# A gated attention and mixer block: token mixing's first product with tokens as the stationary side, and its result turned round by transposes and DRAM

## The chip, the cores and the metric

The kernel runs on one core of one Trainium2 chip. The metric is the device time of one execution in microseconds (us), lower is better. The kernel before takes 911.43 us (median of 3 runs, 911.35 to 912.27).

A core has a matrix engine (PE, with its weight loads shown apart as PEld), a vector engine (DVE), an activation engine (ACT), a general engine (POOL) and a sync engine (SP). In this kernel SP does nothing but issue DMA transfers, one after the other. Every engine works through its own list of instructions in order, and they meet through semaphores: an instruction that waits holds up all that stand behind it on its engine.

## The reference

One input `x` of 2048 tokens by 448 channels goes through attention (16 heads, one shared key and value head) and through a mixer, and a gate adds the two. What matters here is the first half of the mixer, token mixing:

```python
h = _gelu(_layernorm(x, axis=-1) @ w1)
c = D // 4
g0 = jnp.pad(h[:, :, 0*c:1*c], ((0, 0), (1, 0), (0, 0)))[:, :S, :]   # shift +1
g1 = jnp.pad(h[:, :, 1*c:2*c], ((0, 0), (0, 1), (0, 0)))[:, 1:, :]   # shift -1
g2 = jnp.pad(h[:, :, 2*c:3*c], ((0, 0), (2, 0), (0, 0)))[:, :S, :]   # shift +2
g3 = jnp.pad(h[:, :, 3*c:   ], ((0, 0), (0, 2), (0, 0)))[:, 2:, :]   # shift -2
hs = jnp.concatenate([g0, g1, g2, g3], axis=-1) @ w2
x1 = x + hs
...
h2 = _gelu(_layernorm(x1, axis=-1) @ w3) @ w4
```

S is 2048, D is 448 and c is 112. Each quarter of the channels of `h` is moved by one or two tokens before it meets `w2`. All is float32.

## The kernel before, in words

The program has three parts in order of time: token mixing together with the projections of queries, keys and values (to about 124 us), channel mixing with w3 and w4 (to about 400 us), and attention (the rest). The change lies in the first part alone.

Tokens are worked in four blocks of 512 (b = 0 to 3). To keep float32 accuracy at the speed of one pass, each operand is split into a high and a low part (`ah`/`al`, `w1h`/`w1l`, `hh`/`hl`), and a product is made of three, high by high, high by low and low by high. The 448 channels fill three groups of 128 rows and a fourth of 64 that carries another part's rows in its upper half, so a product over the channels takes 11 matmuls (`proj`, lines 129 to 135).

- `stage_q` (u = 0 to 15) projects queries, with keys, values and the gate in spare columns, and sends the result through ACT to DRAM (`q_out`, DRAM tensor `qd`). `stage_kv(b)` issues two loads that bring values back from there (`vT`), and `stage_v` turns all of them by four PE transposes (`vp`) after the first tile of `stage_w2(2)`.
- `stage_w1(b)` makes `h` with channels on the partitions: w1 is the stationary side (112 columns, one quarter m of the channels) and 512 tokens stream past. DVE multiplies the result by the reciprocal deviation of each token. These factors lie along the free dimension, so they have to be spread over the partitions: `ln1_send` transposes them on PE (`rsT`) and writes them to DRAM, `ln1_read` reads them back on 112 partitions (`rsb`). The layernorm's mean is already taken out through w1 (`centre_w1`). ACT then makes the gelu twice, once rounded into `hh` and once in full, and POOL subtracts for `hl`.
- `carry_h(b)` issues seven small DMA transfers on SP that put 16 rows of `hl` at a time into the upper 16 partitions (112 to 127) of `hh` and `hl`, where they save a separate product.
- `stage_w2(b)` makes `hs` for four tiles t of 128 tokens, 11 matmuls each of 448 columns with the tokens of `hh`/`hl` as stationary side, shifted by reading at another offset. DVE adds the result to `x1`. The results rest in two PSUM banks, used in turn (`hs_tile`), so the third tile waits for the first one's addition. The two columns beyond a block come from the next block's `hh` and `hl`, copied by POOL.

`hh` and `hl` have two buffers each. Large temporaries of this part (`xkv`, and later `xn4` and `xt4`) share three buffers under the tag "raw" in turn. During `stage_w2(1)` DVE also makes the layernorm of the first block for channel mixing (`xn4`, turned into `xt4`), `xt_write(0)` sends it to DRAM (`xd`) with four transfers, and `xt_read(0)` brings it back with channels on the partitions (`xr`).

The order on every engine is the order of the code (a manual schedule). For PE it is w1(0), w1(1), w2(0), w1(2), w2(1), q(12 to 15), w1(3), w2(2), w2(3), and then the first w3 group.

Of the kernel before, what the change touches and what calls it, by code (L numbers as in the profile page):

```python
# [37 lines left out]
def f32(ap):  # L38
    return ap.bitcast(F32)
# [3 lines left out]
def gated_mix_kernel(  # L43
# [206 lines left out]
    with tc.tile_pool(name="s1b", bufs=1) as s1b, \  # L250
# [43 lines left out]
        def high_x(b, c0, c1):  # L294
            if b not in xact:
                xact[b] = (s1.tile([P, 4, 512], F32R, tag="ah", bufs=3, name=f"ahk_{b}"),
                           s1.tile([P, 3, 512], F32R, tag="al", bufs=3, name=f"alk_{b}"))
            nc.scalar.copy(xact[b][0][:, c0:c1, :], xraw[b][:, c0:c1, :])

# [61 lines left out]
        rb_of = {}  # L361

# [8 lines left out]

        def ln1_send(b):
            ps = misc_tile(f"rsT_{b}")[0:4, 0:P]
            nc.tensor.transpose(ps, rs1_of.pop(b)[1], ident)
            rT = s1.tile([4, P], F32, tag="rT", bufs=2, name=f"rT_{b}")
            nc.scalar.copy(rT, ps)
            rb_of[b] = dram.tile([4, P], F32, tag="rsd", bufs=2, name=f"rsd_{b}")
            nc.sync.dma_start(rb_of[b], rT)

        def ln1_read(b):  # L380
            rd = rb_of[b]
            rb_of[b] = s1.tile([P, 512], F32, tag="rsb", bufs=2, name=f"rsb_{b}")
            nc.sync.dma_start(rb_of[b][0:C], rd.rearrange("(o t) p -> o (t p)", o=1).broadcast_to([C, 512]))
# [42 lines left out]

        def stage_w1(b, between=None):
            hh[b] = s1b.tile([P, 4, 516], F32R, tag="hh", bufs=2, name=f"hh_{b}")
            hl[b] = s1b.tile([P, 4, 516], F32R, tag="hl", bufs=2, name=f"hl_{b}")
            for tt in (hl, hh):  # L430
                if b == 0:
                    nc.gpsimd.memset(f32(tt[b])[0:C, :, 0:2], 0.0)
                else:
                    nc.gpsimd.tensor_copy(tt[b][0:C, :, 0:2], f32(tt[b - 1])[0:C, :, 512:514])
            for i, m in enumerate(ORDER):
                ps = mm1(f"h_{b}_{m}")
                w = slice(m * C, (m + 1) * C)
                proj(ps[0:C, :], w1h[:, :, w], w1l[:, :, w], *xact[b])
                if between:
# [4 lines left out]
                nc.scalar.activation(hf[0:C, :], hf[0:C, :], AF.Gelu_apprx_tanh)  # L444
                nc.gpsimd.tensor_tensor(hl[b][0:C, m, 2:514], hf[0:C, :], f32(hh[b])[0:C, m, 2:514],
                                        ALU.subtract)
                if i == 1:
                    carry_h(b)
# [58 lines left out]
        ln1_send(0)  # L507
        ln1_read(0)
# [7 lines left out]
        def first(m):  # L516
            low_w2(ORDER[m])
            if m < 2:
                high_w2(ORDER[m + 2])
            else:  # L520
                high_x(3, 2 * m - 4, 2 * m - 2)
            if m == 0:
                ln1_send(1)
                carry_w2(0, 4)
                ln1_read(1)
# [4 lines left out]
        def second(m):  # L530
            if m < 2:
                split_x(3, 2 * m, 2 * m + 2, False)
            else:
                ln1_tile(2, 2 * m - 4)
                ln1_tile(2, 2 * m - 3)

        stage_w1(1, second)
        stage_kv(0)
        stage_kv(1)

# [640 lines left out]
```

## Time and profile before

| what | value |
|---|---|
| median of 3 runs | 911.43 us (911.35 to 912.27) |
| profiled execution, span from first to last instruction | 909.8 us |
| PE busy | 904.0 us, 99% |
| PEld, ACT, DVE, POOL busy | 643.8, 634.5, 543.7, 108.0 us |
| granted TensorE clock | full in all slices |

The three runs are times of the whole execution, and 911.43 is also the middle one of them; the profile gives the span of one execution, which is 1.6 us shorter than that median. Changes in the span are therefore added to the median. In the profile's lists each row has the start in us, the length in us, the engine, the line of the kernel, the operation, what it writes and reads, and how many instructions it merges; a bracket gives how long the engine had been idle before and what ended that. "SPq" and "ACTq" are DMA issues; their length is the time of issuing, not that of the transfer.

### The profile page before, as it was taken

The numbers are of one execution on the slowest core, as the hardware profiler recorded it, in microseconds if no ns is written. First come the engines' busy times: TensorE is split into PE (matmuls) and PEld (weight loads), VectorE is DVE, ScalarE is ACT, GpSimd is POOL, SyncE is SP. The second block draws the span as 40 slices with busy tenths as digits, with TensorE's granted clock in tenths as the row PEclk, the third lists the DMA queues.
The fourth block names the chain that finished last, engine by engine and source line by source line (L and its number), as shares of the span: only waits on it lengthen the run. The fifth ranks groups of instructions, "written<-read, shape, count | busy, mean of one in ns | idle before, by whom it ended". The sixth has DMA issues, their size and how long they took to land.

```text
span 909.8 us, 24136 instructions
## 1 busy us (share of the span) xinstructions
PE 904.0 (99%) x10101; PEld 643.8 (71%) x10101; DVE 543.7 (60%) x1083; ACT 634.5 (70%) x1139; POOL 108.0 (12%) x140
## 2 busy tenths in 40 slices
PE   9999999999999999999999999999999999999998
PEld 7788888888888888875566656556666556666654
DVE  4665264631435736546666666676666667666675
ACT  5542255432131222159999999999999999999996
POOL 3143200212000440002200000000000000000000
PEclk9999999999999999999999999999999999999999
DMA  9822543220222042120000001100011000010001
GB/s 304 296 76 42 162 145 125 39 68 21 39 61 61 16 108 63 29 65 23 26 25 4 26 14 50 30 26 26 3 46 46 26 3 26 14 56 13 15 14 44
DMA packets 41808, 51.81 MB, mean 57 GB/s; under 512 B 9312, under 2 KB 27552, under 8 KB 41696
## 3 DMA queue, kind: packets, MB, share of 16 engines
q1 hardware_dynamic: 38528, 44.54, 17.2%
q10 hardware_dynamic: 3168, 5.70, 1.8%
q8 instruction: 80, 1.31, 0.6%
q14 instruction: 32, 0.26, 0.1%
HBM read 37.04 MB, written 11.93 MB: 54 GB/s over the span
## 4 chain that ended last, share of the span: by engine, by line
PE 99%; ACT 0%; DVE 0%; issue 0%; ACTq 0%; DVEq 0%
PE bank L979 24%; PE bank L942 22%; PE bank L843 8%; PE acc L693 5%; PE acc L692 5%; PE acc L694 5%; PE g L132 4%; PE g L131 4%; PE g L133 4%; PE hs L460 1%; PE hs L461 1%; PE g L135 1%; PE g L134 1%; PE h L131 1%; PE h L132 1%; PE h L133 1%
## 5 line engine op out<-in xcount | busy, mean ns | idle before, releaser
L969 ACT ACTIVATE p<-bank 128x512 f32<-128x512 f32 x762 | 386.9, 615 | 1.6 <-PE bank L942 1.5
L979 PE MATMUL bank<-p,vext 128*32 128x256 f32 x3076 | 244.4, 379 | 0.0
L979 PE MATMUL bank<-pd,vext 128*32 128x256 f32 x1020 | 241.1, 379 | 0.0
L966 DVE COPY pd<-bank 128x512 f32<-128x512 f32 x254 | 175.3, 691 | 51.1 <-PE bank L942 49.6
L979 PEld LDWEIGHTS bank<-p,vext 128*32 128x32 f32 x3076 | 126.4, 110 | 82.2 <-ACT p L969 0.5
L681 ACT ACTIVATE gh<-g 128x512 fp32r<-128x512 f32 x54 | 32.3, 599 | 180.6 <-PE g L135 180.6
L983 DVE TENSOR_TENSOR o<-o,bank 128x256 f32<-128x256 f32 x222 | 93.6, 421 | 91.9 <-ACT p L969 53.9
L974 ACT ACTIVATE pd<-pd 128x1024 f32<-128x1024 f32 x127 | 140.4, 1106 | 0.0
L942 PE MATMUL bank<-qh,kH 30*128 30x512 f32 x1024 | 117.3, 443 | 0.0
L979 PEld LDWEIGHTS bank<-pd,vext 128*32 128x32 f32 x1020 | 111.8, 110 | 0.1
L684 DVE TENSOR_TENSOR gl<-gf,gh 128x512 fp32r<-128x512 f32 x54 | 37.2, 689 | 116.6 <-ACT gf L682 116.5
L942 PE MATMUL bank<-qh,kL 28*128 28x512 f32 x1024 | 104.8, 392 | 0.0
L942 PE MATMUL bank<-ql,kH 28*128 28x512 f32 x1024 | 104.6, 391 | 0.0
L942 PEld LDWEIGHTS bank<-qh,kH 30*128 30x128 f32 x1024 | 60.7, 182 | 56.5 <-ACT p L969 46.0
L693 PE MATMUL acc<-w4l,gh 128*128 128x448 f32 x216 | 78.9, 365 | 0.0
L692 PE MATMUL acc<-w4h,gh 128*128 128x448 f32 x216 | 78.8, 365 | 0.0
L694 PE MATMUL acc<-w4h,gl 128*128 128x448 f32 x216 | 78.7, 364 | 0.0
L843 PE MATMUL bank<-wof,on 128*32 128x224 f32 x1008 | 73.1, 367 | 0.0
L132 PE MATMUL g<-al,w3h 128*128 128x512 f32 x168 | 65.8, 392 | 0.0
L131 PE MATMUL g<-ah,w3h 128*128 128x512 f32 x168 | 65.6, 390 | 0.0
L133 PE MATMUL g<-ah,w3l 128*128 128x512 f32 x168 | 65.5, 390 | 0.0
L942 PEld LDWEIGHTS bank<-ql,kH 28*128 28x128 f32 x1024 | 51.8, 185 | 8.5
(205 smaller groups left out, 1168.7 us busy)
## 6 DMA issues: line engine op xcount, KB each, us to landing
qd<-qf ACTq DMA_DIRECT2D x16, 256.0 KB
qm<-qd SPq DMA_DIRECT2D x16, 256.0 KB
qr<-qd SPq DMA_DIRECT2D x16, 256.0 KB
rb<-rd SPq DMA_DIRECT2D x15, 256.0 KB
x<-in_x_dram SPq DMA_DIRECT2D x4, 896.0 KB
xd<-xt SPq DMA_DIRECT2D x16, 224.0 KB
w34raw<-in_w_dram SPq DMA_DIRECT2D x7, 512.0 KB
w34raw<-in_w_dram SPq DMA_DIRECT2D x7, 448.0 KB
```

The lines of the kernel that those rows point to most:

```text
L131: nc.tensor.matmul(ps, wh[:, c, :], ah[:, c, :], start=(c == 0), stop=False)
L132: nc.tensor.matmul(ps, wh[:, c, :], al[:, c, :], start=False, stop=False)
L133: nc.tensor.matmul(ps, wl[:, c, :], ah[:, c, :], start=False, stop=False)
L692: nc.tensor.matmul(ps, gh[:, tok], w4h[i][:, k, :], start=(f == 0), stop=False)
L693: nc.tensor.matmul(ps, gh[:, tok], w4l[i][:, k, :], start=False, stop=False)
L694: nc.tensor.matmul(ps, gl[:, tok], w4h[i][:, k, :], start=False, stop=(f == stop))
L843: nc.tensor.matmul(ps[32 * j:32 * j + 32, cols], on_of[u][:, tok], wof[:, u % NG, cols], start=start, stop=stop, tile_position=(0, 32 * j))
L942: nc.tensor.matmul(bs[j], w, a, start=(i == 0), stop=(i == 2), tile_position=(32 * j, 0))
L966: nc.vector.tensor_copy(ps[j], bs[j])
L969: behind[kt % 2] = nc.scalar.activation(ps[j], bs[j], AF.Exp, scale=SCALE)
L974: ins = nc.scalar.activation(pd, pd, AF.Exp, scale=SCALE)
L979: nc.tensor.matmul(pv[32 * j:32 * j + 32, q], vext[:, kt, :], p_of[u, kt][j][:, q], start=start, stop=stop, tile_position=(0, 32 * j))
```

## The change

`stage_w1` now takes a tile of 128 tokens as the stationary side (`ah`/`al`) and streams all 448 channels of w1 past it, four tiles per block. Tokens now lie on the partitions, so ACT's gelu takes the reciprocal deviation as its per-partition scale, straight from PSUM; the transposes, the DRAM trip and the DVE multiplication of the factors go away (`ln1_send`, `ln1_read`). The result has tokens on the partitions while `stage_w2` wants channels there. So DVE transposes it in 32 by 32 blocks (`ht`), four transfers write it to DRAM (`hd`), two read it back with channels on the partitions (`hr`), and a new step `split_h(b)` makes `hh` on ACT and `hl` on POOL and issues `carry_h(b)`. `ht` and `hr` use the three "raw" buffers. The order on PE becomes w1(0), w1(1), w1(2), w2(0), w1(3), w2(1), q(12 to 15), w2(2), w2(3).

```diff
         def stage_w1(b, between=None):
+            ah, al = xact[b]
+            rs = rs1_of.pop(b)[1]
+            ht = s1.tile([P, 4, 512], F32, tag="raw", bufs=3, name=f"ht_{b}").rearrange("p c n -> p (c n)")
+            ht = ht[:, 0:4 * D].rearrange("p (f t j) -> p f t j", f=NE, t=4)
+            for t in range(4):
+                ps = mm1(f"h_{b}_{t}")[:, 0:D]
+                tok = slice(t * P, (t + 1) * P)
+                for c in range(3):
+                    nc.tensor.matmul(ps, ah[:, c, tok], w1h[:, c, :], start=(c == 0), stop=False)
+                    nc.tensor.matmul(ps, al[:, c, tok], w1h[:, c, :], start=False, stop=False)
+                    nc.tensor.matmul(ps, ah[:, c, tok], w1l[:, c, :], start=False, stop=False)
+                nc.tensor.matmul(ps, ah[:, 3, tok], w1h[:, 3, :], start=False, stop=False)
+                nc.tensor.matmul(ps, ah[:, 3, tok], w1l[:, 3, :], start=False, stop=True)
+                hf = s1.tile([P, 512], F32, tag="hf", bufs=3, name=f"hf_{b}_{t}")[:, 0:D]
+                nc.scalar.activation(hf, ps, AF.Gelu_apprx_tanh, scale=rs[:, t:t + 1])
+                if between:
+                    between(t)
+                nc.vector.transpose(ht[:, :, t, :], hf.rearrange("p (f j) -> p f j", j=32))
+            hd = dram.tile([NE, 32, 4, 128], F32, tag="hd", bufs=2, name=f"hd_{b}")
+            for p in range(4):
+                nc.sync.dma_start(hd[:, :, p].rearrange("f i u -> i f u"),
+                                  ht[32 * p:32 * p + 32].rearrange("i f t j -> i f (t j)"))
+            hr_of[b] = s1.tile([P, 4, 512], F32, tag="raw", bufs=3, name=f"hr_{b}")
+            rows = hd.rearrange("f i p u -> (f i) (p u)").rearrange("(m c) n -> c m n", c=C)
+            for m0, m1 in ((2, 4), (0, 2)):
+                nc.sync.dma_start(hr_of[b][0:C, m0:m1, :], rows[:, m0:m1, :])
+
+        def split_h(b):
             hh[b] = s1b.tile([P, 4, 516], F32R, tag="hh", bufs=2, name=f"hh_{b}")
             hl[b] = s1b.tile([P, 4, 516], F32R, tag="hl", bufs=2, name=f"hl_{b}")
+            hr = hr_of.pop(b)
...
-            for i, m in enumerate(ORDER):
-                ps = mm1(f"h_{b}_{m}")
-                w = slice(m * C, (m + 1) * C)
-                proj(ps[0:C, :], w1h[:, :, w], w1l[:, :, w], *xact[b])
-                if between:
-                    between(i)
-                hf = s1.tile([P, 512], F32, tag="hf", bufs=3, name=f"hf_{b}_{m}")
-                nc.vector.tensor_mul(hf[0:C, :], ps[0:C, :], rb_of[b][0:C, :])
-                nc.scalar.activation(hh[b][0:C, m, 2:514], hf[0:C, :], AF.Gelu_apprx_tanh)
-                nc.scalar.activation(hf[0:C, :], hf[0:C, :], AF.Gelu_apprx_tanh)
-                nc.gpsimd.tensor_tensor(hl[b][0:C, m, 2:514], hf[0:C, :], f32(hh[b])[0:C, m, 2:514],
-                                        ALU.subtract)
-                if i == 1:
+            for m in ORDER:
+                raw = hr[0:C, m, :].rearrange("n (p t j) -> n p t j", p=4, t=4)
+                hi, lo = [tt[b][0:C, m, 2:514].rearrange("n (t p j) -> n p t j", p=4, t=4) for tt in (hh, hl)]
+                nc.scalar.copy(hi, raw)
+                nc.gpsimd.tensor_tensor(lo, raw, f32(hi), ALU.subtract)
+                if m == 2:
                     carry_h(b)
...
         stage_w1(1, second)
+        split_h(0)
         stage_kv(0)
         stage_kv(1)
-        stage_w2(0, third)
+        stage_w1(2, lambda t: ln1_tile(3, t))
+        split_h(1)
         stage_kv(2)
-        ln1_tile(3, 3)
+        stage_w2(0)
         mv0, rs0 = stats_tiles(s1, "m")
-        stage_w1(2, lambda t: stats_tile(s1, 0, t, mv0))
+
+        def fourth(t):
+            if t == 0:
+                split_h(2)
+            stats_tile(s1, 0, t, mv0)
+
+        stage_w1(3, fourth)
         stats_end(mv0, rs0)
-        ln1_send(3)
-        ln1_read(3)
...
         stage_w2(1, lambda t: layernorm_norm(0, t, mv0, rs0, xn4[:, t, :], xt4))
         xt_write(0, xt4)
+        split_h(3)
         for u in range(12, 16):
             stage_q(u)
         stage_kv(3)
-        stage_w1(3)
```

Two small callbacks change with it. In w1(0) the loads of x for block 3 are no longer split on ACT between the tiles; all of `split_x(3)` (two ACT and three DVE instructions) now stands after the first tile of w1(1), and in the last two tiles of w1(1) DVE makes the statistics of block 2 as before.

The DMA queue on SP from w1(0) to the first transfers of block 2's `carry_h` shows how the transfers of one block now stand among those of another. Number suffixes tell the block first (`hd_1` is block 1's `hd`). Before, the carries of block 0 and block 1 follow each other, and then the value loads:

```order
L418 DMA w2h_132<-w2h_132 16x448
L425 DMA hh_0_423<-hl_0_424 16x512 x2
L425 DMA hl_0_424<-hl_0_424 16x512 x2
L425 DMA hh_0_423<-hl_0_424 16x512 x2
L425 DMA hl_0_424<-hl_0_424 16x512
L425 DMA hh_1_527<-hl_1_528 16x512 x2
L425 DMA hl_1_528<-hl_1_528 16x512 x2
L425 DMA hh_1_527<-hl_1_528 16x512 x2
L425 DMA hl_1_528<-hl_1_528 16x512
L335 DMA vT_134<-qd_81 16x1x512 x4
```

Now the same queue holds, after the same row of w2:

```order
L397 DMA w2h_132<-w2h_132 16x448
L429 DMA hd_0_489<-ht_0_415 32x14x128 x4
L434 DMA hr_0_494<-hd_0_489 112x2x512 x2
L429 DMA hd_1_581<-ht_1_497 32x14x128 x4
L434 DMA hr_1_586<-hd_1_581 112x2x512 x2
L404 DMA hh_0_589<-hl_0_590 16x512 x2
L404 DMA hl_0_590<-hl_0_590 16x512 x2
L404 DMA hh_0_589<-hl_0_590 16x512 x2
L404 DMA hl_0_590<-hl_0_590 16x512
L329 DMA vT_134<-qd_81 16x1x512 x4
L429 DMA hd_2_689<-ht_2_612 32x14x128 x4
L434 DMA hr_2_694<-hd_2_689 112x2x512 x2
```

What moved: `carry_h(0)` stands behind the write and the read of block 1, and every `carry_h` has a write and a read of 0.9 MB ahead of it.

On DVE in w2(1) (the additions L465, later L468, with the layernorm of block 0 between them) this stood before, with what each row waits for in brackets:

```order
L442 TENSOR_TENSOR hf_2_3_797<-h_2_3_782,rsb_2_684 112x512 [waits PE_49,Pool_49]
L465 TENSOR_TENSOR x1_72<-x1_72,hs_1_0_816 128x448 [waits PE_49]
L159 TENSOR_SCALAR xn4_814<-x1_72,mv_s1_m_709,rs_s1_m_710 128x448 [waits Pool_49]
L160 STREAM_TRANSPOSE xt4_815<-xn4_814 128x14x32 [waits DVE_49]
L465 TENSOR_TENSOR x1_72<-x1_72,hs_1_1_831 128x448 [waits PE_49]
```

And this stands there now:

```order
L426 STREAM_TRANSPOSE ht_3_774<-hf_3_3_862 128x14x32 [waits Activation_49]
L468 TENSOR_TENSOR x1_72<-x1_72,hs_1_0_880 128x448 [waits PE_49]
L159 TENSOR_SCALAR xn4_878<-x1_72,mv_s1_m_772,rs_s1_m_773 128x448 [waits DMAHW4_49,DMAHW3_49,DMAHW5_49,DMAHW2_49,DMAHW7_49,DMAHW0_49,Pool_49]
L160 STREAM_TRANSPOSE xt4_879<-xn4_878 128x14x32 [waits DMAHW3_49,DMAHW2_49,DMAHW4_49,DMAHW1_49,DVE_49]
L468 TENSOR_TENSOR x1_72<-x1_72,hs_1_1_895 128x448 [waits PE_49]
```

What moved: the first transpose into `xt4` now waits for four DMA semaphores. They are those of the four writes of `hd_3`, because `xt4` takes the "raw" buffer that `ht_3` had. The next addition of `hs` stands behind it.

More of the change, by code (lines that the diff above doesn't have):

```diff
@@ L370, in ln1_tile @@
                 stats_end(*rs1_of[b])
[L372 to L383, printed above, removed]
         ones = s1.tile([P, P], F32R, name="ones")
```

43 lines of the change are left out of this document (14 added, 29 removed).

## The prediction

> **What bounds the kernel now.** I read the page first (busy shares, the chain of work that ended last), then the timeline of each engine over the first 130 us, and last the windows of that part, cut where PE goes from one stage to the next.
>
> ```profile
> PE 904.0 (99%) x10101; PEld 643.8 (71%) x10101; DVE 543.7 (60%) x1083; ACT 634.5 (70%) x1139; POOL 108.0 (12%) x140
> PE 99%; ACT 0%; DVE 0%; issue 0%; ACTq 0%; DVEq 0%
> 36.51:56.92 20.41, 20.41 (x90) 15.37 (x89) 12.11 (x19) 12.45 (x21) 7.74 (x8) 1.00 0.58 169
> 56.92:66.07 9.15, 9.15 (x47) 8.32 (x45) 5.63 (x14) 2.43 (x5) 3.70 (x7) 1.00 0.14 36
> 66.07:76.28 10.21, 10.21 (x45) 7.58 (x44) 6.26 (x14) 3.80 (x6) 3.86 (x7) 1.00 0.17 47
> 76.28:85.48 9.20, 9.20 (x46) 8.37 (x45) 5.34 (x10) 1.41 (x3) 3.44 (x6) 1.00 0.13 33
> 85.48:95.51 10.03, 10.03 (x45) 8.25 (x44) 1.90 (x4) 1.77 (x3) 0.33 (x2) 1.00 0.69 165
> 95.51:105.72 10.21, 10.21 (x45) 7.70 (x44) 2.08 (x3) 4.38 (x7) 2.36 (x3) 1.00 0.17 52
> 105.72:124.24 18.52, 18.52 (x94) 17.06 (x92) 10.50 (x19) 6.06 (x11) 3.42 (x10) 1.00 0.53 167
> ```
>
> The window rows give start and end, length, then busy time and count of PE, PEld, DVE, ACT and POOL, the granted clock, the DMA share and GB/s. They are w1(0) with w1(1), w2(0), w1(2), w2(1), q(12 to 15), w1(3), and w2(2) with w2(3). PE is busy for the whole length of each. So PE has no slack: what is saved on it is won, and what it waits is lost. The others have room; of them only the hour of delivery counts.
>
> **What PE saves.** w1 takes 20.41 + 10.21 + 10.21 = 40.83 us for 4 x 44 matmuls of 512 columns, 0.232 us each. The new ones are 4 x 44 of 448 columns with 128 weights, the shape of w2. Inside w2(0)'s 9.15 us lies one transpose of factors:
>
> ```profile
> 63.50 0.37 PE L463 MATMUL hs<-w2h,hl 128*128 128x448 f32 x1
> 63.70 0.27 PE L374 MATMUL rsT<-ident,rs_s 128*4 128x128 f32 x1
> 64.02 0.37 PE L461 MATMUL hs<-w2l,hh 128*128 128x448 f32 x1
> ```
>
> From 63.50 to 64.02 two matmuls and the transpose pass, 0.52 us, of which the transpose is about 0.11. So w2 needs (9.15 - 0.11) / 44 = 0.2055 us for one of 448 columns, and w1 will need 176 x 0.2055 = 36.2 us, 4.65 less. Three more transposes outside the w1 windows add 0.33. Together PE saves 5.0 us, if it never waits.
>
> **The chain that comes in.** Before, a finished w1 tile reached `hh` and `hl` through DVE, ACT and POOL. Now block b goes: gelu, DVE transposes, four writes, two reads, ACT copies and POOL subtractions, seven carries, and w2(b) needs the last carry within its first tile. The DMA legs have rows, since `xd`/`xr` of channel mixing has the write's exact shape and `xr` 1.0 MB against 0.9 for the read:
>
> ```profile
> 176.40 3.04 SPq L167 DMA_DIRECT2D xd<-xt  x4
> 182.86 0.38 SPq L172 DMA_DIRECT2D xr<-xd  x1
> 183.29 1.13 SPq L174 DMA_DIRECT2D xr<-xd  x2
> 187.00:188.00 1.00, 1.00 (x7) 0.93 (x6) 0.62 (x1) 0.34 (x1) 0.00 (x0) 1.00 0.96 172
> 55.32 1.15 SPq L425 DMA_DIRECT2D hh<-hl  x2
> 59.05 0.59 SPq L425 DMA_DIRECT2D hl<-hl  x1
> 59.69 2.79 SPq L335 DMA_DIRECT2D vT<-qd  x4
> 65.85 1.33 SPq L335 DMA_DIRECT2D vT<-qd  x2
> 184.46 37.26 SPq L345 DMA_DIRECT2D kf<-qd  x32
> 223.59 0.61 POOL L350 CAST kH<-kf 128x512 fp32r<-128x512 f32 x1 [7.76 <-DMA kf<-qd]
> ```
>
> From the first write's issue to the first read's, which waits for the data, are 6.45 us; two reads take about 1.15 us to issue, and the data is in some 5 us after the first issue (the DMA engines are still full until about 188). Seven carries take 55.32 to 59.64, 4.3 us. A small load's data arrives 2.6 us after its issue begins (the 32 `kf` loads end issue at 184.46 + 37.26 = 221.72, the last began some 0.7 earlier, and POOL starts at 223.59); I take that for the carries too.
>
> The busy times on the way come from these groups:
>
> ```profile
> L681 ACT ACTIVATE gh<-g 128x512 fp32r<-128x512 f32 x2 | 1.2, 599 | 1.8 <-PE g L135 1.8
> L160 DVE STREAM_TRANSPOSE xt<-xn 128x448 f32<-128x448 f32 x4 | 2.6, 645 | 0.1
> L139 DVE BATCH_NORM_STATS2 st_s<-x 128x6 f32<-128x448 f32 x20 | 12.2, 609 | 0.0
> L140 DVE BATCH_NORM_AGGREGATE mv_s<-st_s 128x2 f32<-128x6 f32 x16 | 2.9, 183 | 0.5
> L125 DVE TENSOR_TENSOR alk<-xkv,ahk 128x1024 fp32r<-128x1024 f32 x3 | 3.7, 1244 | 5.2 <-ACT ahk L122 4.9 <-ACT ahk L298 0.3
> L125 DVE TENSOR_TENSOR alk<-xkv,ahk 128x512 fp32r<-128x512 f32 x6 | 4.1, 686 | 6.3 <-ACT ahk L122 6.3
> L122 ACT CAST ahk<-xkv 128x1024 fp32r<-128x1024 f32 x4 | 4.0, 1052 | 1.0 <-DMA xkv<-in_xT_dram 0.6 <-ACT qf L303 0.4
> L465 DVE TENSOR_TENSOR x<-x,hs 128x448 f32<-128x448 f32 x16 | 9.8, 613 | 11.5 <-PE hs L463 11.4
> L618 ACT CAST ah<-xr 128x512 fp32r<-128x512 f32 x4 | 2.2, 618 | 7.5 <-DMA xr<-xd 7.5
> L445 POOL TENSOR_TENSOR hl<-hf,hh 112x512 fp32r<-112x512 f32 x16 | 18.2, 1136 | 41.5 <-ACT hf L444 41.5
> ```
>
> **First wait, at w2(0).** PE starts w1(0) at 36.4 and without a wait ends w1(0), w1(1), w1(2) at 45.5, 54.5, 63.5. w2(0) needs its last carry at 65.6. In w1(1) the first gelu ends at 48.6 and the ACT split of x at 49.65; then DVE has three subtractions (1.24 + 0.69 + 0.69), four transposes at about 0.6 and four statistics at about 0.75, and ends at 57.6, behind the 56.0 that PE alone would allow. Writes of block 1 go out at 57.6 (those of block 0, ready at 47, are done), its reads at 64.05 to 65.2, and only then, since SP takes them in order, `carry_h(0)`: 65.2 to 69.5, the last begun at 68.9 and landed at 71.5. PE waits from 65.6 to 71.5, 5.9 us. If DVE is done at 56.0 the wait is 4.4; if the write meets the previous block's read and takes 1 us more, 7. Block 0's own data is there at 58.6, and POOL done at 62, so this is not what counts. ACT stands at block 0's copies until about 60, while w1(2) fills PSUM banks that are free: no cost.
>
> **Second wait, at w2(1).** From 69.5 SP is a chain without a gap: four `vT` 2.8, writes of block 2 and their wait 6.45, reads 1.15, `carry_h(1)` 4.3, two `vT` 1.3, `carry_h(2)` 4.3. That is 89.8, and the writes of block 3 (ready at 88.9) are done at 96.3. Before that DVE's first transpose into `xt4` can't start, and the second addition of `hs` ends at about 97.7 (0.65 + 0.61). PE ends w2(0)'s first tile at 71.7, the stage at 78.5, w1(3) at 87.5 and three tiles of w2(1) at 94.3; the fourth needs the bank of the second. It waits 3.4 us. Bounds: 2 if DMA is quicker by a microsecond or two, 5.5 if the carries take 5 us each time. It does not add to an error of the first wait, since both ends hang on the carries of block 0. POOL's part (four subtractions of 1.14, then the block's factors) ends near 89 and hides behind w2(1)'s first tile.
>
> **Third wait, at the transposes of v.** Before, w1(3) lay between the last q and w2(2). Now w2(2) follows the last q at once:
>
> ```profile
> 95.28 0.39 PE L135 MATMUL q<-ahk,wql 128*128 128x512 f32 x1
> 96.58 2.82 SPq L335 DMA_DIRECT2D vT<-qd  x2
> 106.71 0.61 SPq L592 DMA_DIRECT2D w34raw<-in_w_dram  x1
> 115.62 2.18 ACT L618 CAST ah<-xr 128x512 fp32r<-128x512 f32 x4 [7.54 <-DMA xr<-xd]
> 107.98 0.60 PE L356 MATMUL vp<-ident,vT 128*128 128x128 f32 x4
> ```
>
> The second `vT` load waits for the last q's store; it ends issue at 99.40 and begins at 98.7, 3.2 us after the last q (95.51), and lands 2.6 later: 5.8. PE wants `vp` after one tile, at 2.3. It waits 3.5 us (2.1 if the load lands in 1.2 us, 4.5 if in 3.6). Behind it on SP the w3/w4 load and `xr` follow at 3.9 and are in 8.9 us later (106.71 to 115.62), 12.8 after q; w2(2) then ends at 12.9, so DVE, which has `xr`'s split ahead of an addition, is late no more than before. Without the wait for `vp` this would be the next in line, at about 3 us: the two don't add.
>
> **Costed at nothing.** Eight ACT gelus per block become four and four copies, DVE multiplications become transposes of the same length; PE's stages cover both. If POOL's subtraction with strided output took twice 1.14 us, carries would move by 1.1 and the first wait not at all.
>
> **Sum.** 911.43 - 5.0 + 5.9 + 3.4 + 3.5 = 919.2. The profiled span, 909.8, would become 917.6; it stands 1.6 below the median.
>
> [...] In the first stretch of the trace the array runs slower:
>
> ```profile
> 1.05 4.39 PE L93 MATMUL warm_ps<-warm 128*128 128x256 bf16 x20 [1.05 <-DVE warm L66]
> ```
>
> That is 0.22 us for 256 columns, half the rate of w1's 0.232 for 512, for 4.4 us. Before, PE has no later gap. If the waits brought this back, 4.4 us at half rate would cost 2.2 each; after the first wait the second one would swallow it, after the second or third it stays, which gives 921.4 to 923.6. [...]
>
> **Rivals and chances.** (1) Forecast, three waits: 0.63, 916 to 922. (2) All hidden, faster: the price is PE's 5.0 alone, 906.4. It decides if the last carry lands before 65.6, or more loosely if the waits sum to under 5; for it speaks that POOL has block 0's data at 62, against it that SP holds the carries behind block 1's trip. 0.06. (3) Only the first wait is real: writes of block 3 land by 92.9 and `vT` by its tile; 912.3, no change that a measurement here could tell (0.2%, 1.8 us). Against it, the DMA legs are measured rows: 0.10. (4) Slower still, by half clock after waits or 0.9 MB transfers that meet each other: 921.4 to 925, 0.21. Faster 0.05, same 0.10, slower 0.85, since a part of (3) lies on either side. The range leaves out (2), the lower part of (3) and the top of (4): 912.8 to 923.5.
>
> **What would show it.** w1 stages near 9.05 us in PE's windows; PE's first idle time before hs of block 0 with a DMA carry `hh<-hl` as releaser, some 6 us; DVE idle before `xt<-xn` ended by `hd<-ht` and PE idle before the fourth hs tile of block 1; PE idle before `vp` with `vT<-qd`. The prediction fails if SP's legs are shorter than 6.45 and 4.3, if the loads land sooner, or if PE's clock falls.

## The result, and the profile after

The changed kernel takes 927.30 us (median of 5 runs, 925.04 to 927.68) against 911.76 for the kernel before (5 runs, 911.35 to 912.27): a ratio of 1.0167, with a 95% interval of 1.0156 to 1.0178. It is 15.5 us slower. The prediction was 919.2 (912.8 to 923.5): slower was right, and the size is twice the predicted one (15.5 against 7.8). The profiled execution is the 925.04 one, 2.3 below its median, with a span of 923.3.

From the page of the changed kernel, the busy time of PE, the granted clock in 40 slices of 23 us, and the chain that ended last:

```profile
PE 903.8 (98%) x10097; PEld 647.6 (70%) x10097; DVE 541.5 (59%) x1083; ACT 632.6 (69%) x1135; POOL 106.4 (12%) x140
PEclk9998989999999999999999999999999999999999
PE 94%; DVE 2%; DMA 2%; ACT 1%; issue 1%; POOL 0%; SPq 0%; DVEq 0%; ACTq 0%; POOLq 0%
```

The chain was PE at 99%; DMA, DVE and ACT now lie on it. The two eights in the clock are new. The windows are cut again where PE goes from stage to stage: w1(0) to w1(2), w2(0), w1(3), w2(1), q(12 to 15), w2(2) with w2(3). Columns as in the prediction.

```profile
36.35:63.10 26.75, 26.75 (x133) 24.80 (x132) 13.61 (x27) 13.28 (x22) 5.57 (x8) 1.00 0.69 180
63.10:81.44 18.34, 11.92 (x46) 10.19 (x45) 5.50 (x12) 2.91 (x5) 6.06 (x10) 0.81 0.61 144
81.44:90.53 9.09, 9.09 (x45) 8.26 (x44) 5.35 (x12) 3.98 (x7) 4.89 (x8) 1.00 0.43 103
90.53:101.98 11.45, 9.34 (x46) 8.26 (x44) 5.20 (x10) 0.64 (x1) 1.22 (x2) 1.00 0.67 151
101.98:111.95 9.97, 9.97 (x45) 8.26 (x44) 1.89 (x4) 3.95 (x7) 5.12 (x10) 1.00 0.77 181
111.95:137.04 25.09, 20.70 (x93) 18.74 (x92) 9.81 (x18) 5.50 (x10) 1.05 (x4) 0.86 0.46 146
```

The w1 stages are as short as predicted: 26.75 + 9.09 = 35.84 us against 40.83. In three windows the length exceeds PE's busy time: PE waits there. And in two of these the busy time itself is too long: w2(0) needs about 9.04 at full clock and shows 11.92, and the last window shows 20.70 against 18.52 before. There the mean clock is 0.81 and 0.86. In the timeline stand the three waits (in brackets how long the engine had been idle, and what ended that), and the transfers and the DVE instruction behind them:

```profile
64.34 1.17 SPq L404 DMA_DIRECT2D hh<-hl  x2
69.89 0.71 PE L464 MATMUL hs<-w2l,hh 128*128 128x448 f32 x1 [6.42 <-issue]
92.07 3.03 SPq L429 DMA_DIRECT2D hd<-ht  x4
98.40 0.65 DVE L160 STREAM_TRANSPOSE xt<-xn 128x448 f32<-128x448 f32 x1 [4.36 <-DMA hd<-ht]
99.61 0.48 PE L463 MATMUL hs<-w2h,hh 112*128 112x448 f32 x1 [2.12 <-DVE x L468]
115.26 1.42 SPq L329 DMA_DIRECT2D vT<-qd  x2
118.75 1.09 PE L350 MATMUL vp<-ident,vT 128*128 128x128 f32 x4 [4.39 <-DMA vT<-qd]
```

All three predicted waits are there, 6.4, 2.1 and 4.4 us (predicted 5.9, 3.4 and 3.5). w3 starts at 137.04, where before it started at 124.24: 12.8 us of the loss arise ahead of that point.

**The clock.** The half clock comes in pieces of one length. Finer windows put the fall behind the first wait at 68.55 and its end at 75.38, and the fall at the third wait at 116.34: two pieces of 6.83 us, and from 68.55 to 116.34 are 14 times 3.413. Cut on that grid, the stretches around the first wait read:

```profile
61.73:65.14 3.41, 1.74 (x9) 1.27 (x7) 2.64 (x7) 0.63 (x1) 0.67 (x1) 1.00 0.43 76
65.14:68.55 3.41, 0.00 (x0) 0.00 (x0) 1.66 (x4) 0.62 (x1) 1.84 (x5) 1.00 1.05 296
68.55:71.97 3.42, 2.08 (x5) 1.58 (x6) 0.00 (x0) 1.66 (x3) 2.66 (x3) 0.50 0.22 36
71.97:75.38 3.41, 3.41 (x11) 3.02 (x10) 0.62 (x1) 0.00 (x0) 1.57 (x4) 0.50 0.68 139
75.38:78.79 3.41, 3.41 (x19) 3.15 (x18) 0.62 (x1) 0.00 (x0) 0.00 (x0) 1.00 0.74 157
```

PE stops at 63.5. The stretch in which it is idle throughout still counts as full clock; the next two run at half, the second of them although PE works through it (11 matmuls instead of 19). Then it is full again.

### The profile page after: what moved, and what is told of

Its sections match the earlier page's. It is cut to its first block, busy times and chain, and to the rows that moved or that the text cites. A ratio compares the mean times of both kernels' runs of the same rounds, so it can differ in the third digit from the quotient of the medians.

```text
span 923.3 us, 24148 instructions
## 1 busy us (share of the span) xinstructions
PE 903.8 (98%) x10097; PEld 647.6 (70%) x10097; DVE 541.5 (59%) x1083; ACT 632.6 (69%) x1135; POOL 106.4 (12%) x140
## 4 chain that ended last, share of the span: by engine, by line
PE 94%; DVE 2%; DMA 2%; ACT 1%; issue 1%; POOL 0%; SPq 0%; DVEq 0%; ACTq 0%; POOLq 0%
PE bank L976 24%; PE bank L939 22%; PE bank L840 7%; PE acc L690 5%; PE acc L689 5%; PE acc L691 5%; PE g L132 4%; PE g L131 4%; PE g L133 4%; PE g L135 1%; PE g L134 1%; PE hs L464 1%; PE hs L463 1%; PE hs L466 1%; PE q L132 1%; PE q L131 1%
## 5 line engine op out<-in xcount | busy, mean ns | idle before, releaser
L131 PE MATMUL g<-ah,w3h 128*128 128x512 f32 x168 | 65.6, 390 | 0.0
```

Of the source, the lines that this page charges most:

```text
L131: nc.tensor.matmul(ps, wh[:, c, :], ah[:, c, :], start=(c == 0), stop=False)
```

## The experiments

Each time stands beside runs of the kernel before on the same chip (medians 911.56 to 912.12). "After" is the changed kernel; the edits are to it unless the text says otherwise. Theory L says that SP's list and the round trips set the pace and the waits hang together; its rival A says that each wait is a loss of its own. Theory C says that the idle gaps cost clock as well.

**After, once more.**

> The changed kernel once more, unchanged. Its first profiled execution took 925.04 us, the other four 926.8 to 927.7, 2.3 us more at the middle, and no trace shows where. If the difference is a fourth stretch of half clock (behind the 2.1 us gap at w2(1), say), a profile of about 927 shows a granted clock of 0.50 there, some 2 us long in its effect. If it is DMA that is later, the gaps are longer and the clock is the same. Time: 925 to 928.

Median 925.67 (924.29 to 927.32), ratio 1.0152 (1.0139 to 1.0166). The profiled execution took 924.29 with the same three waits (6.46, 2.50, 4.59) and one stretch of half clock fewer (two behind the first wait, one at the third). Ten executions of one kernel thus spread over 3.4 us where those of the kernel before spread over 1.4. No trace of a 927 us execution was taken, but the mean granted clock of each is on record. One more stretch of half clock would lower it by some 0.002 (half of 3.41 us in 923, an estimate). Only the slowest execution, 927.68 us, has a lower clock (0.989) than the traced one of 925.04 (0.992); six others, from 925.67 to 927.33, have 0.992 as well. So 2.3 of the 3.4 us lie between executions with as much half clock; what makes them is open.

**PE kept busy in the waits.**

```diff
+        keep_warm("warm_a", 44)      # 44 matmuls of 256 columns, result unread
         stage_w2(0)
...
```

Another 16 stand after w2(1)'s third tile and 28 ahead of vp.

> The three waits stay; PE fills them with small matmuls whose result nobody reads: 44 ahead of w2(0) (about 4.7 us at full clock), 16 after the third tile of w2(1) (1.7 us), 28 ahead of the transposes of v (3.0 us). Theory C (PE's idle gap brings the clock down, and this costs time of its own): no slice after the first 20 us shows less than full clock; the 2.2 us behind the third wait go, and of the 2.9 behind the first only 0.7, since block 3's writes then wait for SP (free at 91.4) instead of w1(3) (92.05). 2.9 us less than the changed kernel. Theory W (the waits alone are longer than forecast, and the clock would be swallowed): the same time, within 0.5 us. If the clock falls for another reason (the matmuls, or a limit of power), it falls in spite of the filling and the time is the same or longer.

924.17, ratio 1.0136 (1.0120 to 1.0151). Its windows of w2(0) (with the filling) and of w2(2) with w2(3):

```profile
63.29:79.30 16.01, 14.31 (x89) 12.65 (x89) 5.49 (x12) 2.92 (x5) 6.07 (x10) 1.00 0.60 138
110.97:134.10 23.13, 21.76 (x122) 19.64 (x120) 9.80 (x18) 5.53 (x10) 1.05 (x4) 1.00 0.50 159
```

The clock stays at 1.00, and hs starts behind the first wait at 70.15, as late as without the filling (69.89): same wait, no loss behind it. w3 starts at 134.10, 2.9 us ahead of the first trace of after and 2.5 ahead of the second, as theory C had it; for the traced execution theory W falls. The medians differ by 1.5 only and the intervals of the ratios overlap: 0.9 went at the end of the program (from the start of the last product to the end of the span are 4.8 us, 3.9 in after), and two of the three other executions have a mean clock of 0.997 against 0.999 of the profiled one, so a stretch of half clock was left in them in spite of the filling.

**SP's order alone.**

```diff
-        stage_w1(1, second)
-        split_h(0)
+        stage_w1(1, second, lambda: split_h(0))   # carries ahead of block 1's writes
```

> SP issues block 0's carries ahead of block 1's writes instead of behind them; nothing else moves. Theory L (SP's list as a whole sets the start of w2(1)'s fourth tile, and the first wait only takes from a wait that would come anyway): w2(0) starts without a wait, but block 1's writes go out at about 63 instead of 57.2, its carries land at 88 while w2(1) wants them at 81.6, PE waits 6.4 us there with the same fall of the clock, block 3's writes go out at 92, and the time is the changed kernel's within 1 us. Theory A (each wait is a loss of its own): the first wait's 6.4 us and the 2.9 us of half clock behind it go, 9 us less.

927.87, ratio 1.0181 (1.0165 to 1.0198): nothing gained, so theory L and not A, though the time is 2.2 us above after's 925.67 and not within 1 us of it. The place was wrong, too. PE's waits in w2(0) and w2(1), and SP's writes of block 1:

```profile
63.88 3.24 SPq L431 DMA_DIRECT2D hd<-ht  x4
79.92 0.74 PE L465 MATMUL hs<-w2h,hh 112*128 112x448 f32 x1 [9.05 <-POOL hh L456]
101.81 0.47 PE L465 MATMUL hs<-w2h,hh 112*128 112x448 f32 x1 [2.19 <-DVE x L470]
```

w2(0) starts without a wait and stops at its last tile, 9.05 us, for the two columns that POOL copies from block 1. Taking the carries out of the way uncovered the next thing with the same trip behind it.

**v's transposes later.**

```diff
         def third(t):
-            if t == 0:
+            if t == 2:
                 stage_v()
```

> The four transposes of v stand behind the third tile of w2(2) instead of the first; nothing else moves. The second vT load landed at 118.75, and the third tile ends at 118.9 if PE does not wait, so the wait of 4.4 us goes and with it 2.2 us of half clock. Theory N (the load of xr is the next in line, as the prediction says): ACT and DVE get xr at 126.2, DVE's addition of w2(3)'s first tile stands behind that, and PE waits about 3 us before the third tile of w2(3); 3.7 us less than the changed kernel. Theory H (xr is hidden): 6.6 us less. If 3 us of waiting brings the clock down again: 1.5 us less.

923.68, ratio 1.0124 (1.0107 to 1.0140), 2.0 less than after. The wait for vT is gone, and xr is next in line as the prediction said:

```profile
100.27 0.48 PE L463 MATMUL hs<-w2h,hh 112*128 112x448 f32 x1 [3.08 <-DVE x L468]
130.69 0.47 PE L463 MATMUL hs<-w2h,hh 112*128 112x448 f32 x1 [2.16 <-DVE x L468]
```

The 2.16 us are followed by a stretch of half clock, and so are the 3.08 of w2(1) in this execution. In the second trace of after a gap of 2.50 us at w2(1) brought none. On the grid of its trace, this kernel's stretch with the gap at w2(3), and the next one:

```profile
128.80:132.21 3.41, 1.52 (x7) 1.43 (x8) 3.34 (x6) 3.36 (x7) 0.00 (x0) 1.00 0.00 0
132.21:135.63 3.42, 3.31 (x9) 2.46 (x8) 3.26 (x7) 0.56 (x1) 0.00 (x0) 0.50 0.62 167
```

And in the second trace of after the two stretches across which the gap of 2.50 lies, on that trace's grid:

```profile
94.51:97.92 3.41, 2.56 (x13) 2.01 (x11) 0.00 (x0) 0.00 (x0) 0.00 (x0) 1.00 0.91 185
97.92:101.33 3.41, 1.76 (x9) 1.63 (x10) 2.94 (x6) 0.00 (x0) 0.00 (x0) 1.00 0.54 159
```

1.89 us idle in one stretch halved the next; 0.85 and 1.65 in two did not.

**Gap length by itself.**

> This kernel computes nothing of the reference: PE runs 56 bursts of 50 to 66 matmuls of 448 columns (10 to 14 us at full clock), and between them it waits for a chain of DVE instructions of growing length, from about 0.6 to about 7 us, the whole row four times. In the traces of the changed kernel and of its variants the half clock lasts 3.41, 6.83 or 10.24 us, multiples of one length, and starts up to 5 us after PE went idle; a gap of 2.50 us brought none and one of 2.16 us did. Theory G (the clock is decided in consecutive stretches of 3.41 us that run by themselves; a stretch that is idle for more than about half of it halves the clock of the next): no fall behind gaps under 1.5 us, always one behind gaps over 3.5 us, and between them it depends on where the gap lies on the grid; all falls start on one grid of 3.413 us. Theory I (an idle time over a fixed limit halves the clock): a sharp limit between 2 and 3 us that does not depend on the place, and falls that start a fixed time after PE went idle.

One execution. All 41 falls between the first gap and the last start on one grid of 3.4133 us, to within 0.003. By length of the gap, the stretches of half clock behind each of the four gaps (three at 7.33; the shortest is 0.65 the first time and 0.74 after):

```
gap us   half-clock stretches
0.65     0 0 0 0
1.01     0 0 0 0
1.54     0 0 0 0
2.06     1 1 1 1
2.59     1 0 0 1
3.11     1 1 1 1
3.64     1 1 2 1
4.17     1 2 1 1
4.69     1 2 2 2
5.22     2 2 1 2
5.75     1 2 2 2
6.27     2 2 2 2
6.80     3 2 2 2
7.33     2 2 3
```

Windows on the grid for a gap of 2.06 in one stretch, then for one of 2.59 across two (PE's busy time is the second number, the clock the third from the end):

```profile
302.87:306.29 3.42, 1.36 (x7) 1.21 (x7) 1.81 (x5) 0.00 (x0) 1.00 0.00 0
306.29:309.70 3.41, 3.41 (x10) 3.00 (x10) 0.00 (x0) 0.00 (x0) 0.50 0.00 0
562.29:565.70 3.41, 1.56 (x8) 1.10 (x6) 1.71 (x5) 0.00 (x0) 1.00 0.00 0
565.70:569.11 3.41, 2.67 (x13) 2.48 (x14) 0.59 (x2) 0.00 (x0) 1.00 0.00 0
```

Theory G: of the four gaps of 2.59, the two that lay across two stretches brought no fall, and the two with 2.05 us or more in one stretch did. At full clock the limit lies near 1.85 idle of 3.41: 1.95 us or more always brought the fall in these runs, 1.85 did not. In the kernels 1.78 did it once and failed once, so the border is not sharp by these modelled times.

**The carries on ACT's queue.**

```diff
-                nc.sync.dma_start(to, src[16 * i:16 * i + 16, 2, 0:512])
+                nc.scalar.dma_start(to, src[16 * i:16 * i + 16, 2, 0:512])   # behind all four copies
```

> The seven carries of each block are issued on ACT's queue, behind the four ACT copies of the block, instead of on SP's; nothing else moves. Theory L (SP's list sets the pace; a block's round trip of writes and reads then hangs on the carries of the block before): w2(0) starts with at most 1.5 us of waiting, waits some 3 us ahead of its last tile for the two columns of block 1 (its data landed at 67.5 to 69.4 and POOL needs until about 73), w1(3) starts near 75 instead of 81, and block 3's writes go out at about 87 instead of 92, held by ACT (block 2's copies and carries stand ahead of its gelus) and no longer by SP; w2(1)'s fourth tile starts near 94.6 instead of 99.6. The wait for vT stays. 5 us less than the changed kernel, give or take 2. Rival A (each wait is a loss of its own): the first wait goes with its half clock, 9 us less. Rival Q (the carries are bound by the transfers, not by the queue that issues them): they land as late as on SP, the same time.

928.29, ratio 1.0177 (1.0163 to 1.0190): 2.6 us slower than after, and none of the theories. SP's writes of blocks 1 and 2:

```profile
57.59 5.86 SPq L429 DMA_DIRECT2D hd<-ht  x4
70.13 6.09 SPq L429 DMA_DIRECT2D hd<-ht  x4
```

They take 5.9 and 6.1 us from the first issue to the last instead of 3.0, each while ACT issues seven carries (59.7 to 64.9, 72.3 to 78.3). The carries did leave SP's list, w2(0)'s second product began at 66.40 instead of 69.89, and the later waits gave it back. ACT's gelus of w1(3) and copies of q also stand behind carries now. What SP waited for within the first four writes (us in total, times, the longest):

```profile
SPq L429 <- DMA hh<-hl: 2.6, 1, 2.6
SPq L429 <- DMA hd<-ht: 1.8, 1, 1.8
```

No single issue is slow: without these two waits the four take 5.86 - 4.4 = 1.5 us. By the trace one wait ended when a carry on ACT's queue had landed, the other when a write of the four had, though no write reads what a carry writes. Why a write waits for a carry, no run shows.

**xt4 in its own buffer.**

```diff
-        xt4 = s1.tile([P, 2048], F32, tag="raw", bufs=3, name="xt4")
+        xt4 = s1.tile([P, 4, 512], F32R, tag="ah", bufs=3, name="xt4")   # viewed as float32
```

> xt4 gets a buffer of the tag "ah" that is free since w1(1), instead of one that block 3's writes are read from; nothing else moves. Theory S (the second wait is a loss of its own, and what follows hangs on it): DVE goes on at 94 instead of 98.4, w2(1)'s fourth tile starts 2.1 to 2.5 us earlier, xt4's writes go out at about 101.5 instead of 103.9, and the wait for vT keeps its length: 2.1 to 2.5 us less than the changed kernel, and up to 1.7 more in executions in which this gap had cost a window of half clock. Theory T (the third wait takes it back): SP has block 3's carries until 114.7 as before, vT lands at 118.75 all the same, and the wait for it grows from 4.4 to 6.6; the same time as the changed kernel.

922.86, ratio 1.0116 (1.0101 to 1.0131), 2.8 less than after's 925.67. The second wait is gone. In the profiled execution the third takes back a part:

```profile
113.44 0.59 SPq L404 DMA_DIRECT2D hl<-hl  x1
114.07 1.42 SPq L329 DMA_DIRECT2D vT<-qd  x2
117.66 1.08 PE L350 MATMUL vp<-ident,vT 128*128 128x128 f32 x4 [5.62 <-DMA vT<-qd]
```

vT now waits for the end of block 3's carries on SP, and PE 5.62 us for vT instead of 4.4 to 4.6. S and T each hold in part. In this execution w3 starts at 136.04, only 0.5 us ahead of the second trace of after (136.56), so this trace doesn't show where the 2.8 us between the medians lie.

**The fixes together, in two orders.** The first takes together what stands in brackets (carries on ACT, own buffer, v's transposes after w2(3)'s third tile, the last vT loads behind xr, block 2's copies behind w1(3)); the second also moves two q stages ahead of w2(0).

> Together: the carries on ACT's queue; block 2's copies behind w1(3) instead of after its first tile; xt4 in a buffer that nobody else needs; the last vT loads behind xr on SP, and the transposes of v behind the third tile of w2(3). The order of PE's stages stays. Theory L: the waits at w2(1) and at v are gone; what stays is some 3 us ahead of w2(0)'s last tile (block 1's columns, which have the round trip behind them and no work on PE to cover it), perhaps with a window of half clock (1.7), and 1 us at w2(3) for xr: the kernel before less 5.0 plus 4 to 6, so 911 to 913. Theory A (the waits were all there is): the kernel before less 5.0, 907.

> As the kernel before it, and two of the four last q stages stand on PE between w1(2) and w2(0), with block 0's copies after the first tile of w1(2). They cover the round trip of block 1 with 5 us of work. Theory L: no wait of more than 1 us is left on PE in this part and the clock stays full; the 5.0 us that the matmuls of 448 columns save come through: 906.5 to 908.5, faster than the kernel before. If a wait for DMA is left all the same: 909 to 912.

919.24 and 919.29, ratios 1.0073 (1.0057 to 1.0089) and 1.0075 (1.0062 to 1.0088): 6.4 us of the loss gone, 7 left. Both miss their forecasts (911 to 913, and 906.5 to 908.5). In the second, PE waits less than 1 us up to 102, and then:

```profile
99.51 9.79 SPq L167 DMA_DIRECT2D xd<-xt  x4
123.59 0.74 PE L462 MATMUL hs<-w2h,hh 112*128 112x448 f32 x1 [7.34 <-DVE x L467]
```

One wait of 7.3 us for xr, with three stretches of half clock. The four writes of `xd` take 9.8 us from the first issue to the last instead of 3.0, while ACT issues block 3's carries. Within them SP waited for this:

```profile
SPq L167 <- DMA hh<-hl: 5.8, 1, 5.8
SPq L167 <- DMA hl<-hl: 2.6, 1, 2.6
```

`xd` reads nothing that a carry writes. Again two waits, 8.4 of the 9.8 us, end by the trace when a carry has landed.

**Out of each other's way, two attempts.** Block 3's carries behind the last q, xr ahead of the weights' load, its split behind w2(3)'s second tile; in the second attempt carries of blocks 0 to 2 on SP again and three q stages ahead of w2(0).

> As the version with two q stages ahead of w2(0), whose only wait was one of 7.3 us in w2(3) with 10.2 us of half clock: xr came late, since the writes of xd took 9.8 us to issue on SP while ACT issued block 3's carries. Here block 3's copies and carries stand behind the last q's copies, xr goes out ahead of the w3/w4 load, and the split of xr stands behind the second tile of w2(3), so that no addition to x1 waits for it. If the collision of the two queues was the cause, xd is out by 103, xr in by 112, PE goes through without a wait at full clock and starts w3 near 121: 907.5 to 909.5. If xr is late all the same, PE waits ahead of w3 instead of in w2(3): 911 to 916.

> As the kernel before it, but the carries of blocks 0 to 2 are on SP again (only block 3's on ACT), and three q stages stand ahead of w2(0) instead of two, since block 0's carries then land at 69.9. If writes and carries that are issued on two queues at once slow each other, the writes take 3.0 us here instead of 5.9, and this is the faster one of the two: 907 to 909. If SP's list is too long instead, block 1's carries or block 3's writes are late and PE waits 1 to 3 us at w2(1) or at w2(2)'s last tile: 909 to 913.

913.89, ratio 1.0022 (1.0013 to 1.0031), and 923.03, ratio 1.0115 (1.0101 to 1.0131). The first is 5.4 us better than the two before, and still 4.4 above its forecast of 907.5 to 909.5: `xd` in 5.9 us, before any of block 3's carries is issued (its last write waits 4.2 us, by the trace until its own first one has landed), a wait of 1.8 for block 3's carries at w2(3) with a stretch of half clock, and w3's second weights late. The second missed altogether. The writes of `hd` do take 3.0 to 3.2 us again with their blocks' carries on SP (those of `xd`, under block 3's carries on ACT, 7.4), but SP's list was too long: block 0's last carry left SP at 74.2, block 3's writes went out at 95.6, and PE waited 2.2, 2.0 and 3.1 us.

**All w1 stages first.**

```diff
+        stage_w1(3)
         ...
         stage_w2(0, ...)
-        stage_w1(3, fourth)
+        split_h(2)
+        stage_q(12)
+        stage_q(13)
         stage_w2(1, ...)
```

> All carries on SP again, as in the changed kernel, and PE's stages in another order: w1(0) to w1(3) without a stop, w2(0), two q stages, w2(1), two q stages, w2(2), w2(3). The value loads of blocks 0 to 2 stand behind block 3's round trip, xt4 has a buffer of its own, xr goes out ahead of the w3/w4 load, the last value loads behind both, and v's transposes behind the third tile of w2(3). Each block's round trip and its carries then have 9 us or more of PE's work between the w1 that makes the block and the w2 that needs it. Theory L (the time lost is the round trip plus SP's list standing uncovered on PE's path): carries of block 0 land at 69.9 and are wanted at 72.4, those of block 1 leave SP at 80.2 and are wanted at 86.4, block 3's writes go out at 80 instead of 92, xd at 97, xr is in by 111; PE waits nowhere for more than 1 us, the clock stays full, w3 starts near 119.5, and the 5.0 us that the matmuls of 448 columns save come through: 906.5 to 908.5. If a wait of 2 us or more is left, it also risks a window of half clock: 909 to 913.

913.08, ratio 1.0014 (1.0005 to 1.0023): 12.6 us less than after, 4.6 above its forecast of 906.5 to 908.5. Two waits are left:

```profile
104.08 0.47 PE L464 MATMUL hs<-w2l,hh 128*128 128x448 f32 x1 [1.81 <-DMA hh<-hl]
119.78 0.47 PE L463 MATMUL hs<-w2h,hh 112*128 112x448 f32 x1 [1.77 <-DVE x L468]
```

The first, with 1.81 us in one stretch, brought a stretch of half clock. Both stand behind six value loads (4.2 us) ahead of block 2's carries on SP.

**Value loads last.** The edit is to the version before; v's transposes also move behind w2(3)'s last tile.

```diff
-        for b in range(3):
-            stage_kv(b)
...
-        stage_kv(3)
+        for b in range(NB):
+            stage_kv(b)
```

> As the version with all w1 stages in front, and all value loads (eight) stand behind xr and the w3/w4 load on SP, v's transposes behind the last tile of w2(3). In that version six of them, 4.2 us of issuing, stood ahead of block 2's carries and then of xd and block 3's carries, and PE waited 1.8 us at w2(2) for carries and 1.8 in w2(3) for xr, with one window of half clock. Theory L: carries of block 2 land at about 98.5, ahead of w2(2) at 100.7; xd is issued at 98.5 to 101.6 instead of 103.0 to 106.3, xr is in at 112 instead of 117; both waits fall under 0.7 us, the clock stays full, and of PE's 5.0 us at least 4 come through: 907 to 908.5, faster than the kernel before. Rival (the loads meet other transfers there, or the last value loads hold w3): 910 to 913, no gain.

910.78, ratio 0.9994 (0.9985 to 1.0003): level with the kernel before, as its rival had it (910 to 913), and not 907 to 908.5. In the profiled execution there is no half clock and no wait for carries; 2.45 and 0.79 us for xr are left, and the 2.45 lie across two stretches of the grid. Twelve executions spread from 909.33 to 913.83; the three fastest have a mean clock of 0.999, the slowest 0.996.

**Block 3's carries on ACT once more.**

> PE's order as in the two versions before (all w1 first). The value loads of blocks 0 to 2 stand in SP's pause between block 3's writes and its reads; block 3's carries are issued on ACT's queue behind the last q's copy, where no writes are being issued; xr goes out as soon as xd has landed; the split of xr stands behind w2(3)'s first tile, with the load of the next weights behind it. In the last version 2.4 and 0.8 us of waiting for xr were left (ACT had it at 114.4). Theory L: xr is in at 111, no addition waits for it, w3 starts near 119.7 instead of 123.0, and the 5.0 us come through but for what w3's second weights cost (0 to 1.5 us): 907 to 908.7, faster than the kernel before. Rival: the carries on ACT slow xd again, xr is in at 114 and w3 starts at 122 or later: 910 to 912.

912.51, ratio 1.0010 (1.0001 to 1.0019): the rival, half a us above its range. The writes of `xd` again, and what follows:

```profile
99.36 8.19 SPq L167 DMA_DIRECT2D xd<-xt  x4
121.10 0.74 PE L465 MATMUL hs<-w2h,hh 112*128 112x448 f32 x1 [4.69 <-DVE x L470]
```

**All carries on SP, four value loads in SP's pause after block 0's reads.** The edit is to the version with the value loads last; the splits and loads of w3 and w4 move back along with the split of xr:

```diff
         stage_w1(0, first)
+        stage_kv(0)
+        stage_kv(1)
...
         def weights(t):
+            if t == 1:
+                ln_split(0, 0, 4)        # before: after w2(2)'s last and w2(3)'s first tile
```

> As the version with the value loads last (level with the kernel before, 3.2 us of waiting for xr left), all carries on SP. Four of the eight value loads go into SP's pause between block 0's reads (issued by 54.5) and block 1's writes (57.7), the other four stay behind the w3/w4 load; the split of xr stands behind w2(3)'s second tile. Theory L: block 1's trip keeps its time, xr is at ACT at 114.4 as before, no addition that PE waits for stands behind it, w3 starts near 119.7 and loses at most 1 us to its second weights: 907 to 909, faster than the kernel before. Rival: the early loads push block 1's trip, or w3 waits for xr or its weights as long as w2(3) did: 910.5 to 912.

908.22 (908.00 to 909.29), ratio 0.9958 (0.9945 to 0.9972): faster than both kernels, and within its forecast of 907 to 909. Its windows of w1(0) to w1(3) and of w2(2) with w2(3), and the clock by slices:

```profile
37.27:72.94 35.67, 35.67 (x177) 33.05 (x176) 17.23 (x35) 16.47 (x28) 9.41 (x15) 1.00 0.68 172
101.45:120.44 18.99, 18.22 (x89) 16.51 (x88) 7.66 (x15) 5.30 (x10) 3.61 (x11) 1.00 0.76 203
PEclk9999999999999999999999999999999999999999
```

From the start of w1(0) to the start of w3 are 120.83 - 37.27 = 83.6 us against 87.7 before: 4.2 of the 5.0 us come through, with 0.8 of waiting ahead of vp. The same matmuls, transposes and round trips thus end up 17.5 us faster than in the changed kernel (925.67), by order and a buffer of its own for `xt4`.

## Why the prediction was right in direction and wrong in size

- **What PE saves: right.** w1 takes 35.84 us, predicted 36.2.
- **First wait: right in size, in part by luck.** 6.42 us against 5.9. PE wanted a carry not "within its first tile", at 65.6, but at its second matmul, 63.5; and the first carry, issued at 64.34 behind block 1's reads, was used only at 69.89, 5.5 us later, where I had taken 2.6. The profile names no releaser there ("issue"); but the value load behind the carries, which waits for the second of block 1's reads (`hr<-hd`), went out at 69.34, so these reads were in only half a us before PE went on. The two errors nearly cancel.
- **Second wait: right in cause, 2.1 instead of 3.4.** PE came later, since the first wait and its half clock had taken 2.9 + 0.5 more than planned. DVE was released by block 3's writes as predicted; these went out at 92.07, right behind the last transpose of `ht` (92.05), not behind SP's list, which would have been free at 91.4. So the fourth tile started at 99.61 and not at 97.7.
- **Third wait: right in cause, 4.4 instead of 3.5.** Store, first load and landing took 6.8 us behind the last q, not 5.8. That xr is next in line, at about 3 us, was right: 2.16 in the experiment.
- **Half clock: the step that failed.** The half rate of the first 4.4 us was priced at 2.2 us, but the sum has no term for it. That the waits would hardly bring it back was my estimate, and no trace before the result showed it; in the run of gaps one of 2.06 us halved the clock four times of four. Half clock lengthened PE's work by 11.92 - 9.04 = 2.9 us behind the first wait and by 20.70 - 18.52 = 2.2 behind the third. What of that reached the end is read from the run with PE kept busy, whose clock stays full:

```profile
90.89 3.23 SPq L435 DMA_DIRECT2D hd<-ht  x4
98.62 0.48 PE L469 MATMUL hs<-w2h,hh 112*128 112x448 f32 x1 [1.50 <-DVE x L474]
```

Block 3's writes went out at 90.89 instead of 92.07 and the fourth tile of w2(1) began at 98.62 instead of 99.61. So the second wait did swallow some 1.9 us of the first half clock, as the prediction expected, and 1.0 came through; the half clock behind the third wait stayed, as it expected too. Together the clock made 2.9 of the 5.0 us by which the start of w3 missed (137.04 against a forecast of 132.0). Rival (4), which had the 0.21, named this cause with 921.4 to 925; the profiled execution ends at its edge, the median above it.

- **The rest of those 5.0 us: waits that were sized too small.** In the run at full clock, too, the fourth tile begins 0.9 us later than the 97.7 forecast, and w2(2) with w2(3) takes 23.13 us where 18.52 + 3.5 = 22.0 were forecast.
- **What is not settled.** The remaining 0.7 us of the profiled execution lie behind w3's start. The median lies 2.3 above it, at the same mean clock of 0.992; where these 2.3 us arise was not traced.

## What to carry to other kernels

A matmul engine that is 99% busy (904.0 of 909.8 us here) hides the delivery times of all others; when a change adds a round trip, list what every queue issues in order, with its pauses, and ask for each stage of PE how much work lies between the one that makes a block and the one that needs it. Removing one wait here mostly uncovered the next with the same queue behind it, and what helped was putting 9 us of other stages over every trip (913.08 us instead of 925.67). Before transfers are moved to another queue, see what else is issued at that time: the four writes took 3.0 us with the carries on SP, and up to 9.8 while ACT issued carries. Price an idle gap of 2 us or more on PE (in the run of gaps 2.06 halved the clock four times of four, 2.59 two) with its half clock, less what a later wait takes back: up to 1.5 us for each stretch of 3.41 us behind it, an estimate from matmuls that start every 0.373 us instead of 0.205.

## What the runs showed of the hardware

- In the traces the granted clock fell stretch by stretch: in the run of gaps all 41 falls lie on one grid of 3.4133 us, to within 0.003. At full clock, 1.95 us or more idle in a stretch always halved the next one in these runs and 1.73 or less never did; between them both were seen. At half clock matmuls of 448 columns started every 0.373 us (71.09 to 74.82 in the first trace of after, ten of them) instead of 0.205, and less idle time kept it low: 0.73 us in a stretch did, 0.60 did not. Gaps of 3.64 to 7.33 us cost one to three stretches.
- Four writes of 224 KB took 3.0 to 3.7 us from the first issue to the last with the carries on SP, and up to 9.8 in the runs that issue carries on ACT. Of the 9.8 us the trace puts 8.4 down to waits that ended when carries had landed (5.8 and 2.6). No run shows why a write waits for a carry.
- A carry issued right behind 0.9 MB of reads on the same queue was in use only 5.5 us after its issue, 0.5 us after the reads were in, against the 2.6 us taken for a small load.
